# A convolution accumulated in PSUM banks, and half of a token mix moved from GpSimd to ScalarE

## The chip, the cores and the metric

The kernel runs on 1 core of one Trainium2 chip. The metric is device microseconds of one execution. Three runs of the kernel before took 1332.1, 1333.57 and 1333.91 us; the median is 1333.57 us.

## The reference

Three layers follow each other, all in fp32, on 8 batches of 576 tokens and 512 channels:

```python
scores = 0.125 * q @ k^T                        # 8 batches, 8 heads, 576 tokens, 64 wide
scores = where(scores >= max(scores) - tau, scores, -1e9)
x = softmax(scores) @ v                         # heads joined: 8 x 576 x 512

x_prev = x shifted by one token                 # first layer behind attention ("MoE 1")
xk = mu_k * x + (1 - mu_k) * x_prev
xr = mu_r * x + (1 - mu_r) * x_prev
v  = relu(xk @ w_k) ** 2 @ w_v                  # 512 -> 1024 -> 512
y  = sigmoid(xr @ w_r) * v

gate = sigmoid(sum over 5 taps of conv_w[k] * y shifted by 4 - k tokens)   # second layer
out  = (gate * (y @ w_val)) @ w_out
```

## The kernel before, in words

Channels lie on partitions, tokens along the free dimension. Behind attention the tokens of all batches (each padded by 4 zero columns) form one row of 4640, cut into 10 blocks of TW = 464. A block has KD = 4 chunks of 128 channels. Every matrix product is fp32 in three passes: each operand is split into a high part, rounded by ScalarE, and a low part (value minus high), subtracted on GpSimd (mostly) or VectorE; TensorE adds weight-high by data-high, weight-low by data-high and weight-high by data-low. So one product of a chunk with KD inputs is 12 matmuls of 464 columns, and a block of the second phase has 12 such products: four each with `w_r`, `w_val` and `w_out` (all at L549).

The first phase is attention with the products of `w_k` and `w_v` woven in. The second phase does, for each block of 464 tokens (`block2`):

- load `xt` (one buffer). For each chunk the shifted part of the mix `xf = omu * x_prev` on GpSimd (L596, in `shift_mix`), then `xf = mu * x + xf` on VectorE (L600, a SCALAR_TENSOR_TENSOR), the high part `xrh` on ScalarE (L611), the low part `xrl` on GpSimd (L614);
- four products with `w_r`; ScalarE takes the sigmoid out of PSUM into `gate` (L796);
- `y = gate * vt` on VectorE (L801), `yh` on ScalarE (L807), `yl` on GpSimd (L810);
- the convolution, for each chunk: tap 0 on ScalarE into the SBUF tile `gate` (L837), four taps on VectorE that read and write `gate` in place (L841), the sigmoid on ScalarE in place (L846);
- four products with `w_val` from `yh`, `yl`; VectorE multiplies the PSUM result by `gate` (L863); `gvh` on ScalarE (L869), `gvl` on GpSimd (L872);
- four products with `w_out`; ScalarE copies them out of PSUM (L888) and a DMA stores them.

PSUM has eight banks, named g0 to g7 in the second phase. Before, only TensorE writes them, and a product takes a free bank.

Nothing is ordered by hand. `Plan` records every operation with its engine, an assumed duration, its dependencies, a priority key (in units of one batch of attention) and tokens, which stand for buffers and banks that it takes and gives back. `Plan.order` plays this through once and so fixes, when the program is built, the order of the instructions on each engine. On the chip each engine runs its list strictly in order and waits on semaphores. A table of numbers (L148 to L165) sets the keys: how early score products, loads, mixes, taps and products are ranked.

Of the kernel before, what the change touches and what calls it, by code (L numbers as in the profile page):

```python
# [8 lines left out]
F32 = mybir.dt.float32  # L9
# [44 lines left out]
class Plan:  # L54
# [90 lines left out]

EARLY, QK_EARLY, T_LATE, EV_EARLY, AV_LATE = 0.1561, 0.0601, 0.0174, 4.8151, 0.1504  # L148
S3_CHUNKS = 54
MOE_LAG = 0.7824  # L150
MOE_STEP = 0.8138
KSTAGE = 4
KBUFS, XKBUFS = 10, 4
GATES = {"a": 1, "b": 3}
XRS = {"a": 1, "b": 1}
MIX_EARLY, SIDE_EARLY = 0.0845, -0.0305
W_KEY, W_STEP = 1.8064, 1.9807
V_KEY, V_STEP = 0.4408, 0.2458
R_AHEAD = 0
HOP = 240.0  # L160
VAL_LAG, OUT_LAG = -2.0743, 4.7957
LATE2, LOAD2, MIX2, CONV_LAG, THR_EARLY = 0.3053, 6.8806, 5.0887, 9.6459, 0.8081
MIX_AT = 133.6317
GUARD_POOL = 15
OUT_FETCH = 3.9825  # L165

SAME = {"dve": 130.0}
ENGINES = ("dma", "pe", "dve", "act", "pool", "none")
# [3 lines left out]
def body(ctx, tc, qka, qkb, vp, w_k, w_v, w_r, w_val, w_out, conv_w, par, out):  # L172
# [381 lines left out]
    def product(w, a, m, K, parts, prio, rel=(), cap=("mm",), each=()):  # L554


        t = {}

        def ps():
            return t["ps"]  # L560
        o = None
        for run, uses, first, end in mm3(ps, w, a, m, list(range(K))):
            def go(run=run, first=first):
                if first:
                    t["ps"] = bank(t["op"])
                run()
            deps = [o] + [parts[kc][at] for kc, at in uses]
            if first:
                deps += W_done[w][m // 4 * K:m // 4 * K + K]
                deps += [h for h, *_ in parts]  # L570
                if cap:
                    deps.append(last.get("m1"))
            o = op("pe", 198 * len(uses), go, deps, prio, acq=cap + (BANKS,) if first else (),
                   rel=(rel if end else ()) + sum((tuple(each) for _, at in uses if at), ()))
            if first:
                t["op"] = o
                if cap:
                    chain("m1", o)
        return o, ps, cap + (t["op"],)

    xm = {}

    def shift_mix(w, src, prio, tiles, pool_, tag, toks, eng, opened=None):

        t, parts, ends = {}, [], []
        for c in range(KD):
            f = {}
            got, ps = src(c), []  # L590
            o = None
            for x, (get, at, k, deps) in enumerate(got):
                def prev(c=c, f=f, get=get, at=at, k=k, x=x):
                    if x == 0:
                        f["f"] = pool_().tile([128, TW], F32, name="xf", tag="xf", bufs=2)
                    nc.gpsimd.tensor_scalar(out=f["f"][:, at:at + k], in0=get()[:, 0:k], scalar1=omu[w][:, c:c + 1],  # L596
                                            scalar2=1.0, op0=ALU.mult, op1=ALU.mult)

                def mix(c=c, f=f, get=get, at=at, k=k):
                    nc.vector.scalar_tensor_tensor(out=f["f"][:, at:at + k], in0=get()[:, 1:1 + k],  # L600
                                                   scalar=mu[w][:, c:c + 1], in1=f["f"][:, at:at + k],
                                                   op0=ALU.mult, op1=ALU.add)
# [133 lines left out]
    def after_first():  # L736
# [5 lines left out]
               rel=BANKS[4:] + ("mm", "mm"))  # L742
    end_1 = op("none", 0, after_first, v_kept[-KD:] + [W_done["v"][-1]] + W_done["out"], 0)
    tokens.update(xt=1, axr=XRS["a"], bxr=XRS["b"], rxf=2, agate=GATES["a"], bgate=GATES["b"],
                  vt=2, y=2, yh=2, gv=2, o=3)
    fetch_weight("r", end_a, -2)
    fetch_weight("val", end_a, -1)
    fetch_weight("out", end_1, B + MOE_LAG + OUT_FETCH)
# [1 line left out]
    def block2(n, base):  # L750
# [26 lines left out]
        def xr_tiles(c):  # L777
            if c == 0:
# [1 line left out]
            return [x[:, c, :] for x in t["xr"]]  # L780
        get, parts, ends = shift_mix("r", lambda c: [(lambda: t["xt"][:, c, :], 0, TW, (lx,))], se + MIX2, xr_tiles,
                                     lambda: pool["a"], "xr",
                                     ("rxf", lambda c: () if c else (xr_at + "xr",)), R_LO, xr_ready[xr_at])
        op("none", 0, lambda: None, [e[-1] for e in ends], 0, rel=("xt",))


# [1 line left out]
        for m in range(KD):  # L788
# [20 lines left out]
            def lo(m=m):  # L809
# [5 lines left out]
            o = chain("ymul", op("dve", 554, mul, (o, lv, last.get("ymul"), end_1), pr - LATE2,  # L815
                                 acq=("y",) if m == 0 else (), rel=("vt",) if m == KD - 1 else ()))
            h = chain("yh", op("act", 497, hi, (o, last.get("yh")), pr - LATE2, acq=("yh",) if m == 0 else ()))
            l = op("pool", 1155, lo, (h,), pr - LATE2)
# [14 lines left out]
        for c in range(KD):  # L833
            pr = base + CONV_LAG + c * u

            def tap0(c=c):
                nc.scalar.activation(out=t["gate"][:, c, :], in_=t["y"][:, c, 0:TW], func=AF.Copy,  # L837
                                     scale=cw[:, c, 0:1])

            def tap(c=c, k=1):  # L840
                nc.vector.scalar_tensor_tensor(out=t["gate"][:, c, :], in0=t["y"][:, c, k:k + TW],  # L841
                                               scalar=cw[:, c, k:k + 1], in1=t["gate"][:, c, :],
                                               op0=ALU.mult, op1=ALU.add)

# [108 lines left out]
```

## Time and profile before

| | |
|---|---|
| median of three runs | 1333.57 us (1332.1 to 1333.91) |
| the profiled execution | 1332.2 us, of it 1330.4 us from the first to the last instruction (the span) |
| busy share of the span | TensorE 94%, VectorE 77%, ScalarE 61%, GpSimd 59% |
| mean granted TensorE clock | 0.976 of full speed |
| HBM traffic | 95 GB/s over the span |

[...] The share over the whole span is a mean over stages with different limits, so the views below are cut by stage.

### The profile page before, as it was taken

The page shows a single profiled execution, that of the slowest core. Times are in us where ns is not written, and L with a number is a line of the kernel's source. Part 1 is how long each engine was busy: PE and PEld are TensorE (multiplying, and loading weights), DVE is VectorE, ACT ScalarE, POOL GpSimd, SP SyncE. Part 2 cuts the span into 40 slices and gives each one's busy share as a digit, 9 for nine tenths or more (in the row PEclk, how much of TensorE's full clock was granted, in tenths as well). Part 3 has the DMA queues.
Part 4 walks back from the last instruction along what each step waited for, and adds up shares of the span by engine and source line. Part 5 has one row for each costly group of instructions (what it writes and reads, how often), then busy time and mean ns, then how long its engine had stood idle before and what let it go on. Part 6 is the DMA issues. An engine that isn't in the chain of part 4 may idle for free.

```text
span 1330.4 us, 21096 instructions
## 1 busy us (share of the span) xinstructions
PE 1250.3 (94%) x7104; PEld 1046.7 (79%) x7104; DVE 1018.5 (77%) x2078; ACT 817.0 (61%) x1568; POOL 783.9 (59%) x1001
## 2 busy tenths in 40 slices
PE   5787999999999999999999999999998788999998
PEld 4565778877888778878888888888886677888887
DVE  7999898798797797888796886854419999776540
ACT  6888877676677676776775776653324443445442
POOL 6999767556566666457565465441217776565422
PEclk8889999999999999999999999999999888999999
DMA  6442422433323233224332212004124212221112
GB/s 233 126 143 84 137 74 69 147 105 101 111 78 123 85 110 113 83 74 128 101 125 86 77 65 80 20 24 179 58 90 148 80 61 96 91 86 58 43 43 100
DMA packets 51339, 127.57 MB, mean 96 GB/s; under 512 B 8608, under 2 KB 26144, under 8 KB 50464
## 3 DMA queue, kind: packets, MB, share of 16 engines
q1 hardware_dynamic: 51232, 126.23, 28.6%
q8 instruction: 57, 0.93, 0.3%
q14 instruction: 50, 0.41, 0.1%
HBM read 91.48 MB, written 34.73 MB: 95 GB/s over the span
## 4 chain that ended last, share of the span: by engine, by line
PE 53%; DVE 20%; POOL 9%; issue 8%; ACT 6%; DMA 3%; SPq 0%; POOLq 0%; DVEq 0%; ACTq 0%
PE g L549 31%; PE s L408 8%; PE g L513 7%; PE g L464 6%; DVE gate L841 4%; DVE p L434 4%; DVE sm L417 2%; PE g L516 2%; ACT p L430 2%; DVE xf L600 2%; POOL yl L810 2%; POOL p L447 2%; DVE kl L363 1%; DVE k L660 1%; POOL gvl L872 1%
## 5 line engine op out<-in xcount | busy, mean ns | idle before, releaser
L447 POOL TENSOR_SCALAR p<-p,sm 128x576 f32<-128x576 f32 x288 | 239.1, 834 | 159.9 <-DVE sm L444 75.9
L434 DVE SCALAR_TENSOR_TENSOR p<-s,sm,p 128x576 f32<-128x576 f32 x288 | 231.0, 811 | 47.3 <-ACT p L430 34.3
L417 DVE TENSOR_REDUCE sm<-s 128x1 f32<-128x576 f32 x288 | 213.8, 749 | 58.8 <-PE s L408 56.2
L430 ACT ACTIVATE p<-s,sm 128x576 f32<-128x576 f32 x288 | 213.2, 750 | 73.6 <-DVE sm L417 49.8
L408 PE MATMUL s<-qkh 128*128 128x288 f32 x640 | 209.6, 341 | 26.7 <-DVE p L434 17.4
L464 PE MATMUL g<-par_t,p 128*128 128x128 f32 (+1 forms) x1312 | 185.5, 278 | 24.7 <-POOL p L447 14.5
L464 PEld LDWEIGHTS g<-par_t,p 128*128 128x128 f32 (+1 forms) x1312 | 152.7, 141 | 41.3 <-POOL p L447 26.4
L408 PE MATMUL s<-kl,qkh 128*128 128x288 f32 x640 | 184.0, 301 | 0.9 <-DVE kl L363 0.9
L420 POOL TENSOR_SCALAR sm<-sm,gs 128x1 f32<-128x1 f32 x288 | 114.1, 398 | 119.5 <-DVE sm L417 76.6
L475 ACT ACTIVATE pt<-g 128x512 f32<-128x512 f32 x256 | 144.5, 606 | 26.4 <-PE g L464 26.2
L408 PEld LDWEIGHTS s<-qkh 128*128 128x128 f32 x640 | 123.9, 194 | 45.7 <-DVE p L434 15.9
L841 DVE SCALAR_TENSOR_TENSOR gate<-y,cw_t,gate 128x464 f32<-128x464 f32 x160 | 139.2, 922 | 15.5 <-ACT gate L837 15.1
L513 PE MATMUL g<-pt,v 128*64 128x320 f32 (+1 forms) x1024 | 142.7, 421 | 0.1
L408 PEld LDWEIGHTS s<-kl,qkh 128*128 128x128 f32 x640 | 124.6, 195 | 6.4 <-DVE kl L363 1.5
L549 PE MATMUL g<-xkh,w_k_hi 128*128 128x464 f32 x320 | 123.0, 384 | 0.2 <-ACT pt L475 0.2
L549 PE MATMUL g<-kh,w_v_hi 128*128 128x464 f32 x320 | 121.6, 380 | 0.0
L549 PE MATMUL g<-xkh,w_k_lo 128*128 128x464 f32 x320 | 119.1, 372 | 0.0
L549 PE MATMUL g<-kh,w_v_lo 128*128 128x464 f32 x320 | 119.1, 372 | 0.0
L513 PEld LDWEIGHTS g<-pt,v 128*64 128x64 f32 x1024 | 69.4, 139 | 56.7 <-issue 13.7
L369 POOL TENSOR_TENSOR qkh<-raw,qkh 64x576 fp32r<-64x576 f32 x64 | 94.8, 1481 | 11.3 <-ACT qkh L359 6.0
L614 POOL TENSOR_TENSOR xrl<-xf,xrh 128x464 fp32r<-128x464 f32 x40 | 59.0, 1490 | 65.8 <-ACT xrh L611 65.8
L810 POOL TENSOR_TENSOR yl<-y,yh 128x464 fp32r<-128x464 f32 x40 | 54.0, 1356 | 66.1 <-ACT yh L807 66.1
(99 smaller groups left out, 2679.7 us busy)
## 6 DMA issues: line engine op xcount, KB each, us to landing
raw<-in_qkb SPq DMA_DIRECT2D x32, 640.0 KB, 4.0
raw<-in_qka SPq DMA_DIRECT2D x32, 608.0 KB, 3.8
v<-in_vp SPq DMA_DIRECT2D x32, 320.0 KB, 3.2
x_d<-x SPq DMA_DIRECT2D x32, 290.0 KB, 3.6
v_d<-vo SPq DMA_DIRECT2D x40, 232.0 KB, 2.0
vt<-v_d SPq DMA_DIRECT2D x10, 928.0 KB, 4.6
stage<-in_w_v SPq DMA_DIRECT2D x8, 512.0 KB, 3.9
wst<-in_w_k SPq DMA_DIRECT2D x8, 512.0 KB, 6.0
```

The costliest lines, as they stand in the source:

```text
L369: nc.gpsimd.tensor_tensor(out=t["hi"][lo_rows, qs], in0=t["raw"][lo_rows, qs], in1=t["hi"][lo_rows, qs].bitcast(F32), op=ALU.subtract)
L408: nc.tensor.matmul(s_t[g][:, hh, 0:NT], lhsT=q, rhs=k, start=(i == 0), stop=(i == len(terms) - 1))
L417: nc.vector.tensor_reduce(out=sm[:, 0:1], in_=s_t[g][:, :, 0:NT], op=ALU.min, axis=AX.XY)
L420: nc.gpsimd.tensor_scalar(out=sm_t[g][:, 1:2], in0=sm_t[g][:, 0:1], scalar1=tau_t, scalar2=1.0, op0=ALU.add, op1=ALU.mult)
L430: nc.scalar.activation(out=view(), in_=s_t[g][:, :, 0:NT], func=AF.Exp, bias=sm_t[g][:, 0:1], scale=-1.0)
L434: nc.vector.scalar_tensor_tensor(out=view(), in0=s_t[g][:, :, 0:NT], scalar=sm[:, 1:2], in1=view(), op0=ALU.is_le, op1=ALU.mult, accum_out ...
L447: nc.gpsimd.tensor_scalar(out=view(), in0=view(), scalar1=sm_t[g][:, 3:4], scalar2=1.0, op0=ALU.mult, op1=ALU.mult)
L464: nc.tensor.transpose(ps[0:w, i * 128:(i + 1) * 128], in_=p_t[pi, j][:, p0:p0 + w], identity=ident)
L475: nc.scalar.activation(out=pt[:, head, :, q0:q0 + 128], in_=ps.rearrange("p (k q) -> p k q", k=4), func=AF.Copy)
L513: nc.tensor.matmul(acc[h * 64:h * 64 + 64, 0:n], lhsT=v[:, kc * 128 + h * 64:kc * 128 + h * 64 + 64], rhs=pt[:, h, kc, 0:n], start=(kc == ...
L549: nc.tensor.matmul(ps()[:, 0:TW], lhsT=W[w][wt][:, kc, m * 128:(m + 1) * 128].bitcast(F32R), rhs=a(at, kc), start=(i == 0 and x == 0), sto ...
L841: nc.vector.scalar_tensor_tensor(out=t["gate"][:, c, :], in0=t["y"][:, c, k:k + TW], scalar=cw[:, c, k:k + 1], in1=t["gate"][:, c, :], op0 ...
```

## The change

Two things in the second phase change their place.

- The convolution. Tap 0 writes a PSUM bank instead of `gate`, the four taps on VectorE read and write that bank in place, and the sigmoid reads the bank and writes `gate`. Each chunk's chain takes a bank token and one of `cv` = 3 tokens, and gives them back behind the sigmoid.
- The mix for `xr`. The shifted part is an activation with a scale on ScalarE that writes a PSUM bank, no longer a GpSimd instruction that writes `xf`; VectorE reads `xt` and that bank and writes `xf`. It takes a bank token and one of `xp` = 2 tokens until VectorE is done. The mix for `xk` in the first phase stays as it was.

The assumed durations of four operations and the table of keys change too, so the order on every engine is another one.

```diff
-S3_CHUNKS = 54
-MOE_LAG = 0.7824
+S3_CHUNKS = 45
+MOE_LAG = 0.7323
+CVB = 3
 ...
-    R_LO = {"pool": 1155}
+    R_LO = {"pool": 1300}
 ...
-    def shift_mix(w, src, prio, tiles, pool_, tag, toks, eng, opened=None):
+    def shift_mix(w, src, prio, tiles, pool_, tag, toks, eng, opened=None, psum=False):
 ...
                 def prev(c=c, f=f, get=get, at=at, k=k, x=x):
+                    if psum:
+                        f["p"] = bank(f["op"])[:, 0:TW]
+                        nc.scalar.activation(out=f["p"], in_=get()[:, 0:k], func=AF.Copy, scale=omu[w][:, c:c + 1])
+                        return
 ...
                 def mix(c=c, f=f, get=get, at=at, k=k):
+                    if psum:
+                        f["f"] = pool_().tile([128, TW], F32, name="xf", tag="xf", bufs=2)
                     nc.vector.scalar_tensor_tensor(out=f["f"][:, at:at + k], in0=get()[:, 1:1 + k],
-                                                   scalar=mu[w][:, c:c + 1], in1=f["f"][:, at:at + k],
+                                                   scalar=mu[w][:, c:c + 1], in1=f["p"][:, at:at + k],
                                                    op0=ALU.mult, op1=ALU.add)
 ...
+                if psum:
+                    o = f["op"] = chain("mix", op("act", 497, prev, first + [last.get("mix")], prio, acq=(BANKS, "xp")))
+                    ps.append(chain("mixd", op("dve", 130 + 1.04 * k, mix, (o, last.get("mixd")), prio, acq=toks[:1],
+                                               rel=(o, "xp"))))
+                    continue
 ...
-                  vt=2, y=2, yh=2, gv=2, o=3)
+                  vt=2, y=2, yh=2, gv=2, o=3, cv=CVB, xp=2)
 ...
-            def tap0(c=c):
-                nc.scalar.activation(out=t["gate"][:, c, :], in_=t["y"][:, c, 0:TW], func=AF.Copy,
-                                     scale=cw[:, c, 0:1])
+            def tap0(c=c, f=f):
+                f["ps"] = bank(f["op"])[:, 0:TW]
+                nc.scalar.activation(out=f["ps"], in_=t["y"][:, c, 0:TW], func=AF.Copy, scale=cw[:, c, 0:1])
 
-            def tap(c=c, k=1):
-                nc.vector.scalar_tensor_tensor(out=t["gate"][:, c, :], in0=t["y"][:, c, k:k + TW],
-                                               scalar=cw[:, c, k:k + 1], in1=t["gate"][:, c, :],
+            def tap(c=c, k=1, f=f):
+                nc.vector.scalar_tensor_tensor(out=f["ps"], in0=t["y"][:, c, k:k + TW],
+                                               scalar=cw[:, c, k:k + 1], in1=f["ps"],
                                                op0=ALU.mult, op1=ALU.add)
 
-            def sig2(c=c):
-                nc.scalar.activation(out=t["gate"][:, c, :], in_=t["gate"][:, c, :], func=AF.Sigmoid)
-            o = op("act", 574, tap0, (hd,), pr)
+            def sig2(c=c, f=f):
+                nc.scalar.activation(out=t["gate"][:, c, :], in_=f["ps"], func=AF.Sigmoid)
+            o = f["op"] = op("act", 574, tap0, (hd, last.get("tap0")), pr, acq=(BANKS, "cv"))
+            last["tap0"] = o
             for k in range(1, 5):
-                o = op("dve", 612, lambda c=c, k=k: tap(c, k), (o,), pr)
-            gates.append(op("act", 497, sig2, (o,), pr))
+                o = op("dve", 612, lambda c=c, k=k, tap=tap: tap(c, k), (o,), pr)
+            gates.append(op("act", 447, sig2, (o,), pr, rel=(f["op"], "cv")))
```

VectorE's list at the start of the second phase, from its first multiplication `y` on, before (L801 is `y`, L841 a tap, L600 the mix, L863 the multiplication of a `w_val` product by `gate`; the number behind a name is the buffer):

```order
L801 TENSOR_TENSOR y_11393<-gate_11214,vt_11367 128x464 x4
L801 TENSOR_TENSOR y_11444<-gate_11437,vt_11397 128x464
L841 SCALAR_TENSOR_TENSOR gate_11214<-y_11393,cw_t_87,gate_11214 128x464 x2
L600 SCALAR_TENSOR_TENSOR xf_11476<-xt_11424,par_t_83,xf_11476 128x464
L600 SCALAR_TENSOR_TENSOR xf_11484<-xt_11424,par_t_83,xf_11484 128x464
L841 SCALAR_TENSOR_TENSOR gate_11214<-y_11393,cw_t_87,gate_11214 128x464 x6
L600 SCALAR_TENSOR_TENSOR xf_11525<-xt_11424,par_t_83,xf_11525 128x464
L863 TENSOR_TENSOR gate_11214<-g0_11432,gate_11214 128x464
```

And the same place now (L813 is `y`, L855 a tap, L607 the mix, L878 the multiplication by `gate`; a name that begins with g0 to g7 is a PSUM bank):

```order
L813 TENSOR_TENSOR y_11403<-gate_11224,vt_11368 128x464 x4
L855 SCALAR_TENSOR_TENSOR g6_11452<-y_11403,cw_t_87,g6_11452 128x464
L855 SCALAR_TENSOR_TENSOR g5_11454<-y_11403,cw_t_87,g5_11454 128x464
L607 SCALAR_TENSOR_TENSOR xf_11473<-xt_11411,par_t_83,g3_11463 128x464
L855 SCALAR_TENSOR_TENSOR g6_11452<-y_11403,cw_t_87,g6_11452 128x464
L607 SCALAR_TENSOR_TENSOR xf_11491<-xt_11411,par_t_83,g0_11471 128x464
L813 TENSOR_TENSOR y_11495<-gate_11435,vt_11438 128x464
L855 SCALAR_TENSOR_TENSOR g6_11452<-y_11403,cw_t_87,g6_11452 128x464
L813 TENSOR_TENSOR y_11495<-gate_11435,vt_11438 128x464
L607 SCALAR_TENSOR_TENSOR xf_11524<-xt_11411,par_t_83,g1_11493 128x464
```

Of block 0's taps eight stood ahead of the third mix of block 2; now three stand there, and the `y` of block 1 have moved up between them. Two taps' banks and two mixes' banks are held at the same time.

ScalarE's list at its first taps 0, before (L837 is tap 0, L611 `xrh`, L846 the sigmoid of the convolution, L796 the sigmoid of a `w_r` product, L869 `gvh`):

```order
L837 ACTIVATE gate_11214<-y_11393,cw_t_87 128x464 x4
L611 ACTIVATE xrh_11497<-xf_11476 128x464
L611 ACTIVATE xrh_11497<-xf_11484 128x464
L846 ACTIVATE gate_11214<-gate_11214 128x464 x2
L796 ACTIVATE gate_11437<-g7_11417 128x464
L611 ACTIVATE xrh_11497<-xf_11525 128x464
L869 ACTIVATE gvh_11550<-gate_11214 128x464 x2
```

And now (L852 is tap 0, L597 the shifted part of the mix, L808 the sigmoid of a `w_r` product, L623 `xrh`, L819 `yh`):

```order
L852 ACTIVATE g6_11452<-y_11403,cw_t_87 128x464
L852 ACTIVATE g5_11454<-y_11403,cw_t_87 128x464
L597 ACTIVATE g3_11463<-xt_11411,omu_t_88 128x464
L597 ACTIVATE g0_11471<-xt_11411,omu_t_88 128x464
L808 ACTIVATE gate_11435<-g1_11429 128x464
L852 ACTIVATE g4_11480<-y_11403,cw_t_87 128x464
L623 ACTIVATE xrh_11488<-xf_11473 128x464
L597 ACTIVATE g1_11493<-xt_11411,omu_t_88 128x464
```

The four taps 0 of a block no longer stand together, and the shifted part of the mix, which waits for the load of `xt`, stands in ScalarE's list between them and the sigmoids.

## Rows read from the trace of the kernel before

**Rows 1.** Windows: engines' busy us (instructions), granted clock, DMA share, GB/s, by stage.

```profile
core 0: us, PE busy (x) PEld busy (x) DVE busy (x) ACT busy (x) POOL busy (x), PEclk, DMA share, GB/s
0.00:140.00 140.00, 104.35 (x610) 76.93 (x611) 125.21 (x293) 110.40 (x210) 119.28 (x166) 0.88 0.45 150
140.00:989.00 849.00, 832.19 (x5075) 696.72 (x5074) 656.72 (x1512) 558.65 (x1084) 470.63 (x674) 1.00 0.28 91
989.00:1010.00 21.00, 19.07 (x87) 15.68 (x87) 11.74 (x11) 10.47 (x19) 15.64 (x14) 1.00 0.79 293
1010.00:1120.00 110.00, 89.55 (x365) 74.73 (x364) 107.52 (x114) 47.57 (x89) 80.14 (x64) 0.88 0.21 70
1120.00:1326.20 206.20, 205.16 (x975) 182.69 (x973) 117.31 (x151) 89.34 (x168) 98.19 (x84) 1.00 0.21 72
1326.20:1330.40 4.20, 0.01 (x1) 0.00 (x0) 0.00 (x0) 0.56 (x1) 0.00 (x0) 0.85 0.29 113
```

**Rows 2.** Chain of waits, long pieces: start us, us, what.

```profile
1211.32 114.91 PE g L549 x549
```

**Rows 3.** Waits of TensorE, 950 to 1331 us: us in total, times, longest.

```profile
PE g L549 <- ACT yh L807: 17.3, 9, 3.5
PE g L549 <- POOL xrl L614: 3.4, 3, 2.1
```

**Rows 4.** Timeline of TensorE from 1056 us: start, us, instruction, idle before.

```profile
1057.32 0.48 PE L549 MATMUL g<-yh,w_val_hi 128*128 128x464 f32 x1 [2.03 <-ACT yh L807]
1061.52 0.76 PE L549 MATMUL g<-yh,w_val_hi 128*128 128x464 f32 x1 [3.51 <-ACT yh L807]
1064.01 0.59 PE L549 MATMUL g<-yh,w_val_hi 128*128 128x464 f32 x1
```

**Rows 5.** Single lines: duration ns min/median/max, first and last start us.

```profile
L841 DVE SCALAR_TENSOR_TENSOR gate<-y,cw_t,gate x160: 682/696/1678, 1006.7 to 1280.5; 128x464 f32<-128x464 f32 x160
L801 DVE TENSOR_TENSOR y<-gate,vt x40: 626/1510/1629, 996.9 to 1267.0; 128x464 f32<-128x464 f32 x40
L863 DVE TENSOR_TENSOR gate<-g,gate x40: 621/628/643, 1017.1 to 1281.9; 128x464 f32<-128x464 f32 x40
L660 DVE TENSOR_TENSOR k<-k x80: 614/642/2014, 155.4 to 966.0; 128x464 f32<-128x464 f32 x80
```

**Rows 6.** Timeline of VectorE and of GpSimd from 1021 us.

```profile
1021.36 4.67 DVE L841 SCALAR_TENSOR_TENSOR gate<-y,cw_t,gate 128x464 f32<-128x464 f32 x3
...
1022.44 1.55 POOL L614 TENSOR_TENSOR xrl<-xf,xrh 128x464 fp32r<-128x464 f32 x1
1023.96 1.58 POOL L810 TENSOR_TENSOR yl<-y,yh 128x464 fp32r<-128x464 f32 x1
```

**Rows 7.** Timeline of VectorE where GpSimd rests.

```profile
1246.63 1.92 DVE L841 SCALAR_TENSOR_TENSOR gate<-y,cw_t,gate 128x464 f32<-128x464 f32 x3
```

**Rows 8.** Windows of the taps alone (L841): VectorE busy, clock, DMA.

```profile
1010.00:1120.00 110.00, 67.23 (x66) 0.88 0.21 70
```

**Rows 9.** Windows of the mix alone (L600).

```profile
1010.00:1120.00 110.00, 18.34 (x17) 0.88 0.21 70
```

**Rows 10.** Windows of y alone (L801).

```profile
1010.00:1120.00 110.00, 16.67 (x15) 0.88 0.21 70
```

**Rows 11.** Windows of the multiplication by gate alone (L863).

```profile
1010.00:1120.00 110.00, 9.73 (x16) 0.88 0.21 70
```

**Rows 12.** Groups: names, shapes, count | busy us, mean ns | idle before.

```profile
L837 ACT ACTIVATE gate<-y,cw_t 128x464 f32<-128x464 f32 x40 | 24.6, 671 | 4.7 <-POOL y L826 4.1 <-POOL y L824 0.5
L596 POOL TENSOR_SCALAR xf<-xt,omu_t 128x464 f32<-128x464 f32 x40 | 38.6, 976 | 13.9 <-DMA xt<-x_d 13.9
```

**Rows 13.** Windows of the shifted part alone (L596): GpSimd busy, clock, DMA.

```profile
1010.00:1120.00 110.00, 18.41 (x18) 0.88 0.21 70
```

**Rows 14.** The first product of the first phase (last figures: first, last start).

```profile
L549 PE MATMUL g<-xkh,w_k_hi x320: 366/372/615, 144.1 to 963.8; 128*128 128x464 f32 x160
```

More of the change, by code (lines that the diff above doesn't have):

```diff
@@ L144, in order @@
         return out
-EARLY, QK_EARLY, T_LATE, EV_EARLY, AV_LATE = 0.1561, 0.0601, 0.0174, 4.8151, 0.1504
-S3_CHUNKS = 54
-MOE_LAG = 0.7824
-MOE_STEP = 0.8138
+EARLY, QK_EARLY, T_LATE, EV_EARLY, AV_LATE = 0.3412, 0.191, -0.1043, 3.5787, 0.083
+S3_CHUNKS = 45
+MOE_LAG = 0.7323
+MOE_STEP = 0.7954
 KSTAGE = 4
 KBUFS, XKBUFS = 10, 4
+CVB = 3
 GATES = {"a": 1, "b": 3}
 XRS = {"a": 1, "b": 1}
-MIX_EARLY, SIDE_EARLY = 0.0845, -0.0305
-W_KEY, W_STEP = 1.8064, 1.9807
-V_KEY, V_STEP = 0.4408, 0.2458
+MIX_EARLY, SIDE_EARLY = 0.5595, -0.1137
+W_KEY, W_STEP = 1.1719, 2.4131
+V_KEY, V_STEP = 1.1249, 0.0151
 R_AHEAD = 0
 HOP = 240.0
-VAL_LAG, OUT_LAG = -2.0743, 4.7957
-LATE2, LOAD2, MIX2, CONV_LAG, THR_EARLY = 0.3053, 6.8806, 5.0887, 9.6459, 0.8081
-MIX_AT = 133.6317
+VAL_LAG, OUT_LAG = 2.0619, 5.0024
+LATE2, LOAD2, MIX2, CONV_LAG, THR_EARLY = 1.1014, 10.4631, -0.7218, 10.0024, 0.6737
+MIX_AT = 334.259
 GUARD_POOL = 15
-OUT_FETCH = 3.9825
+OUT_FETCH = 4.3504
 SAME = {"dve": 130.0}
@@ L572, in product @@
                     deps.append(last.get("m1"))
-            o = op("pe", 198 * len(uses), go, deps, prio, acq=cap + (BANKS,) if first else (),
+            o = op("pe", 210 * len(uses), go, deps, prio, acq=cap + (BANKS,) if first else (),
                    rel=(rel if end else ()) + sum((tuple(each) for _, at in uses if at), ()))
@@ L593, in prev @@
                 def prev(c=c, f=f, get=get, at=at, k=k, x=x):
+                    if psum:
+                        f["p"] = bank(f["op"])[:, 0:TW]
+                        nc.scalar.activation(out=f["p"], in_=get()[:, 0:k], func=AF.Copy, scale=omu[w][:, c:c + 1])
+                        return
                     if x == 0:
-                        f["f"] = pool_().tile([128, TW], F32, name="xf", tag="xf", bufs=2)
+                        f["f"] = f["p"] = pool_().tile([128, TW], F32, name="xf", tag="xf", bufs=2)
                     nc.gpsimd.tensor_scalar(out=f["f"][:, at:at + k], in0=get()[:, 0:k], scalar1=omu[w][:, c:c + 1],
@@ L782, in block2 @@
                                      lambda: pool["a"], "xr",
-                                     ("rxf", lambda c: () if c else (xr_at + "xr",)), R_LO, xr_ready[xr_at])
+                                     ("rxf", lambda c: () if c else (xr_at + "xr",)), R_LO, xr_ready[xr_at], psum=True)
         op("none", 0, lambda: None, [e[-1] for e in ends], 0, rel=("xt",))
@@ L814, in block2 @@
             pr = base + m * u
-            o = chain("ymul", op("dve", 554, mul, (o, lv, last.get("ymul"), end_1), pr - LATE2,
+            o = chain("ymul", op("dve", 900, mul, (o, lv, last.get("ymul"), end_1), pr - LATE2,
                                  acq=("y",) if m == 0 else (), rel=("vt",) if m == KD - 1 else ()))
@@ L834, in block2 @@
             pr = base + CONV_LAG + c * u
-            def tap0(c=c):
-                nc.scalar.activation(out=t["gate"][:, c, :], in_=t["y"][:, c, 0:TW], func=AF.Copy,
-                                     scale=cw[:, c, 0:1])
-            def tap(c=c, k=1):
-                nc.vector.scalar_tensor_tensor(out=t["gate"][:, c, :], in0=t["y"][:, c, k:k + TW],
-                                               scalar=cw[:, c, k:k + 1], in1=t["gate"][:, c, :],
+            f = {}
+            def tap0(c=c, f=f):
[4 more added lines that the diff above has]
+                                               scalar=cw[:, c, k:k + 1], in1=f["ps"],
                                                op0=ALU.mult, op1=ALU.add)
-            def sig2(c=c):
-                nc.scalar.activation(out=t["gate"][:, c, :], in_=t["gate"][:, c, :], func=AF.Sigmoid)
-            o = op("act", 574, tap0, (hd,), pr)
+            def sig2(c=c, f=f):
+                nc.scalar.activation(out=t["gate"][:, c, :], in_=f["ps"], func=AF.Sigmoid)
+            o = f["op"] = op("act", 574, tap0, (hd, last.get("tap0")), pr, acq=(BANKS, "cv"))
+            last["tap0"] = o
             for k in range(1, 5):
-                o = op("dve", 612, lambda c=c, k=k: tap(c, k), (o,), pr)
-            gates.append(op("act", 497, sig2, (o,), pr))
+                o = op("dve", 612, lambda c=c, k=k, tap=tap: tap(c, k), (o,), pr)
+            gates.append(op("act", 447, sig2, (o,), pr, rel=(f["op"], "cv")))
         last["ydone"] = gates + [p_[1] for p_ in yparts]
```

## The prediction

> **What bounds the kernel now.** I read the windows by stage first [rows 1]. From 140 to 989 us, attention with the first layer, TensorE is busy 832.19 of 849 us at full clock: bound by TensorE, and the change can win little there. From 1120 to 1326.2 us it is busy 205.16 of 206.2: bound by it too. Two stages lose time. In the first 140 us TensorE has 104.35 us of work at clock 0.88, while VectorE (125.21) and GpSimd (119.28) are nearly full. And from 1010 to 1120 us, the start of the second phase, VectorE is busy 107.52 of 110 us and TensorE 89.55 at clock 0.88.
>
> What would that last stage take if nothing held TensorE? The chain of waits has a stretch of 549 second-phase matmuls in 114.91 us without a pause [rows 2], 0.2093 us each. The 365 matmuls of the stage make 76.4 us of that; it takes 110. So 33.6 us are lost: 110 - 89.55 = 20.4 us idle, and 89.55 - 76.4 = 13.1 us of slower matmuls. The waits name the holder: TensorE waits 17.3 us for `yh` [rows 3], which ScalarE makes from VectorE's `y`. The timeline shows two such waits, of 2.03 and 3.51 us, and behind them matmuls of 0.59 us where 0.37 is the median of others [rows 4, 14]: the clock goes down after TensorE has stood still.
>
> Why is VectorE full? A tap takes 0.682 us at least and up to 1.678; `y` 0.626 to 1.629, with a median of 1.510; but the multiplication by `gate`, which has one of its two tensors in PSUM, never leaves 0.621 to 0.643 [rows 5]. The timeline shows the reason: three taps take 4.67 us while GpSimd runs two subtractions of 1.55 and 1.58 us beside them [rows 6], and three taps take 1.92 us where GpSimd rests [rows 7]. A VectorE instruction with two tensors in SBUF waits for GpSimd's to end; one with a tensor in PSUM does not.
>
> **The change part by part.** All sums are against the profiled execution, 1332.2 us of which 1330.4 are the span; that is 1.4 us below the median of the runs shown, 1333.57.
>
> Taps. In the stage 66 taps take 67.23 us [rows 8], 1.02 each. Now each has one tensor in SBUF and one in PSUM and does not meet GpSimd. Undisturbed, three in a row take 1.92 us, the last one's 0.70 (the median of all) in it, so (1.92 - 0.70) / 2 = 0.61 from start to start [rows 5, 7]. A PSUM input adds little: 0.628 for the multiplication by `gate` against at least 0.614 for the same operation from SBUF [rows 5], 14 ns. No row shows VectorE writing PSUM, or reading and writing one bank at once. Bounds: 0.61 below, since each column still passes, and above the 1.02 of today, as if it read and wrote the bank in turns. I take 0.63, near the row that shares an operand in PSUM: 66 x 0.63 = 41.6 us.
>
> [...]
>
> Mix. 17 take 18.34 us [rows 9]; at 0.63 they make 10.7. `y` keeps two SBUF tensors and still meets GpSimd: 16.67 us for 15 [rows 10], left as it is, though GpSimd will be there less. The multiplication by `gate` keeps its 9.73 us [rows 11].
>
> VectorE's sum for the same work: 41.6 + 10.7 + 16.7 + 9.7 = 78.7 us instead of 107.5. TensorE needs 76.4. So the stage is balanced, and the larger is 78.7 us. The lists stay strictly in order, and `y`, mixes and taps are handed over between three engines; I allow 5 us for those gaps and for what clock they cost. The stage falls from 110 to 84 us: **-26 us**.
>
> ScalarE. 17 shifted parts come to it, with the form of tap 0, 0.671 us from SBUF to SBUF [rows 12]: 17 x 0.671 = 11.4 us on top of 47.57, 59 of 84 us, 70%. Writes of ScalarE into PSUM are not in the trace; even at 1 us each it would be 64.6 us, so the throughput is covered, the order not (rivals). GpSimd loses 18.41 us in the stage [rows 13] and keeps 61.7 of 84.
>
> Rest of the second phase. 989 to 1010 idles 1.9 us and 1120 to 1326 idles 1.0 [rows 1]: nothing to win, unchanged. The last 4.2 us, copying out and the store, stay.
>
> First phase. None of its operations changes, but its order does. The first product of `w_k`, today at 144.1 us [rows 14], moves in the list from behind 52 of 288 score chunks to behind 47; 144.1 / 52 = 2.8 us per chunk, so it comes 14 us earlier. TensorE runs at 104.35 / 140 = 75% there, and at less than full clock, so up to a quarter of the 14 us is saved if VectorE can feed it: I take **-3 us**, between +2 (VectorE is full there, and the splitting of weights still has to be done before) and -6.
>
> Sum: 1332.2 - 26 - 3 = 1303 us for an execution like the profiled one, 1304.5 with the 1.4 us to the median. I say 1304.
>
> **The rivals.**
>
> *Half of it is eaten by the order* (12%). The stage needs VectorE 78.7 and TensorE 76.4 us, so neither has slack, and every time one list waits for another it is lost on both. The lists show that `y` of block 2 on and the mixes stand between single taps of two or three chains. If it costs 15 to 25 us instead of 5, the result is 1314 to 1324. Against it: outside this stage VectorE has 43% slack, so nothing accumulates.
>
> *Taps in PSUM are no faster* (8%). At the upper bound 1.02, and with mixes as today, VectorE's sum is 67.3 + 18.3 + 26.4 = 112 us, and the stage stays at 110. What is left is the 3 us of the first phase and small change: 1328 to 1336. For it: no row shows the operation. Against it: a row with a PSUM input is steady at 0.628.
>
> *Banks and ScalarE become the bound: slower* (10%). Before, only products hold banks, and in the list a bank comes round after 6 or more products. Now up to 3 chains and 2 mixes hold one each, and 37 of the 120 second-phase products take a bank that was used two or three products, 5 to 7.5 us, before. Such a product starts only when the mix, the multiplication or the sigmoid that held its bank is through its in-order list. The shifted part also brings a wait along: GpSimd waited 13.9 us for the load of `xt` [rows 12]; on ScalarE the sigmoids, `yh` and `gvh` of all other blocks queue behind it, and TensorE waits for those. It would cost all through the second phase, 1340 matmuls or 112 products from 1010 us on. The gain of 29 us is gone at 0.26 us a product; at 0.4 us it is 1332 - 29 + 45 = 1348. Against it: ScalarE and VectorE are below 60% busy after 1120 us [rows 1], so both come to an evacuation soon. [...]
>
> *More than forecast* (4%): `y` gains too. With GpSimd's load down, 15 `y` at 0.63 save 7 us, and the first phase its 6: below 1292.
>
> **How the numbers follow.** The forecast has 66%, with a range of its own of 1292 to 1316 (gaps 0 to 14 us, first phase +2 to -6). For this kernel 0.2%, 2.7 us, is what can be told from no change. Faster: 66 + 12 + 4 and 3 of the 8 of dear taps, 85%. Within 0.2%: 4 of those 8. Slower: the 10 and the last 1, 11%. The range for 8 in 10 goes from 1291 over the half-eaten case to 1331, which leaves out the slower cases and the tails.
>
> **What would show it.** Right: taps at 0.69 to 0.72 us with a maximum near it, mixes the same, `y` still up to 1.6; between 1010 and 1120 us TensorE above 95% and the clock at 1.00; the second phase, from the last `w_v` product to the end, about 315 us instead of the 341 from 989 on; the first product of `w_k` near 130 us. Wrong: taps over 1 us without GpSimd beside them (second rival); TensorE's waits naming ScalarE's sigmoids or VectorE's multiplications, spread to the end (third); or a first phase that ends later than 989 us.

## The result and the profile after

The changed kernel takes 1295.98 us (median of four runs, 1294.72 to 1297.26) against 1332.84 (1332.1 to 1333.91) for the kernel before on the same chip: a ratio of 0.972, 95% interval 0.9706 to 0.974. It is faster, by 8 us more than the 1304 forecast, and inside the range of 1291 to 1331. The profiled execution took 1296.9 us, its span 1295.1.

First the windows by stage of the changed kernel, cut as in [rows 1]; the stage of 110 us that lost time is now gone by 1090.

```profile
core 0: us, PE busy (x) PEld busy (x) DVE busy (x) ACT busy (x) POOL busy (x), PEclk, DMA share, GB/s
0.00:140.00 140.00, 105.26 (x609) 77.64 (x611) 124.28 (x280) 110.14 (x209) 118.19 (x164) 0.91 0.44 145
140.00:991.00 851.00, 831.64 (x5068) 699.28 (x5065) 651.10 (x1533) 564.78 (x1092) 466.07 (x662) 1.00 0.28 92
991.00:1010.00 19.00, 19.00 (x90) 16.45 (x89) 10.37 (x14) 12.21 (x23) 11.54 (x10) 1.00 0.82 316
1010.00:1090.00 80.00, 79.85 (x381) 71.19 (x381) 77.84 (x125) 60.61 (x117) 54.17 (x49) 1.00 0.34 116
1090.00:1291.00 201.00, 200.92 (x963) 180.25 (x961) 87.67 (x137) 87.82 (x169) 76.89 (x69) 1.00 0.19 67
```

In the 80 us from 1010 on TensorE runs 381 matmuls at a granted clock of 1.00 and idles 0.15 us; before, 365 took 110 us at clock 0.88. VectorE is still 97% busy there, but now TensorE sets the pace. The first two rows read much as before.

The waits of TensorE between 950 us and the end are down to one, where [rows 3] had 17.3 us behind `yh` alone:

```profile
PE g L550 <- POOL xrl L626: 0.2, 1, 0.2
```

and the chain of waits ends in one piece, the second phase's matmuls without a pause:

```profile
1017.06 273.87 PE g L550 x1309
```

That is 0.2092 us each, the rate that [rows 2] had in its own free stretch. Single lines of VectorE and ScalarE (duration min/median/max in ns), to be laid beside [rows 5]; L855 is a tap, L607 the mix, L813 `y`, L878 the multiplication by `gate`, L597 the shifted part, now on ScalarE:

```profile
L855 DVE SCALAR_TENSOR_TENSOR g<-y,cw_t,g x160: 687/699/707, 1005.3 to 1233.0; 128x464 f32<-128x464 f32 x160
L607 DVE SCALAR_TENSOR_TENSOR xf<-xt,par_t,g x40: 680/690/700, 934.2 to 1159.2; 128x464 f32<-128x464 f32 x40
L813 DVE TENSOR_TENSOR y<-gate,vt x40: 629/643/1629, 999.2 to 1216.5; 128x464 f32<-128x464 f32 x40
L878 DVE TENSOR_TENSOR gate<-g,gate x40: 624/642/645, 1015.4 to 1261.0; 128x464 f32<-128x464 f32 x40
L597 ACT ACTIVATE g<-xt,omu_t x40: 632/638/653, 930.7 to 1138.9; 128x464 f32<-128x464 f32 x40
```

The four lines that touch PSUM spread over 21 ns at most from the shortest to the longest. `y`, which still has two tensors in SBUF, alone keeps the long tail to 1629 ns; its median fell from 1510 to 643 without its own instruction having changed (the new order does most of that, as the experiments show). The timeline shows VectorE and GpSimd side by side (start us, duration, engine, line, count, idle time before in brackets):

```profile
1025.70 0.92 DVE L813 TENSOR_TENSOR y<-gate,vt 128x464 f32<-128x464 f32 x1
1026.54 0.69 DVE L855 SCALAR_TENSOR_TENSOR g<-y,cw_t,g 128x464 f32<-128x464 f32 x1
1027.15 1.03 DVE L813 TENSOR_TENSOR y<-gate,vt 128x464 f32<-128x464 f32 x1
1032.58 1.91 DVE L855 SCALAR_TENSOR_TENSOR g<-y,cw_t,g 128x464 f32<-128x464 f32 x3
...
1024.93 2.75 POOL L626 TENSOR_TENSOR xrl<-xf,xrh 128x464 fp32r<-128x464 f32 x2 [0.20 <-ACT xrh L623]
1031.44 2.35 POOL L822 TENSOR_TENSOR yl<-y,yh 128x464 fp32r<-128x464 f32 x2 [1.65 <-ACT yh L819]
1033.76 1.19 POOL L626 TENSOR_TENSOR xrl<-xf,xrh 128x464 fp32r<-128x464 f32 x1
```

Three taps run in 1.91 us beside GpSimd's subtractions, as three did before only where GpSimd rested [rows 6, 7]; each of the two `y` beside such subtractions is stretched. The same holds over all 160 taps when the two engines' rows are laid over each other: before, the 55 taps that took over 1.1 times the shortest all overlapped a GpSimd instruction; now 74 taps overlap one and none takes more than 707 ns.

### The profile page after: what moved, and what is told of

It is laid out like the page before. It is cut to its first block, busy times and chain, and to the rows that moved or that the text cites. A ratio compares the mean times of both kernels' runs of the same rounds, so it can differ in the third digit from the quotient of the medians.

```text
span 1295.1 us, 21071 instructions
## 1 busy us (share of the span) xinstructions
PE 1236.7 (95%) x7104; PEld 1044.8 (81%) x7104; DVE 951.3 (73%) x2086; ACT 836.1 (65%) x1608; POOL 726.9 (56%) x953
## 5 line engine op out<-in xcount | busy, mean ns | idle before, releaser
L448 POOL TENSOR_SCALAR p<-p,sm 128x576 f32<-128x576 f32 x288 | 242.2, 845 | 154.0 <-DVE sm L445 89.9
L409 PE MATMUL s<-qkh 128*128 128x288 f32 x640 | 209.8, 342 | 31.3 <-DVE p L435 20.0
L465 PE MATMUL g<-par_t,p 128*128 128x128 f32 (+1 forms) x1312 | 189.2, 277 | 17.6 <-POOL p L448 11.8
L421 POOL TENSOR_SCALAR sm<-sm,gs 128x1 f32<-128x1 f32 x288 | 120.4, 420 | 119.0 <-DVE sm L418 72.5
L409 PEld LDWEIGHTS s<-qkh 128*128 128x128 f32 x640 | 124.2, 194 | 50.0 <-DVE p L435 22.5
L476 ACT ACTIVATE pt<-g 128x512 f32<-128x512 f32 x256 | 147.4, 604 | 25.0 <-PE g L465 24.0
L550 PE MATMUL g<-kh,w_v_hi 128*128 128x464 f32 x320 | 124.8, 390 | 2.4 <-ACT pt L476 2.2
L626 POOL TENSOR_TENSOR xrl<-xf,xrh 128x464 fp32r<-128x464 f32 x40 | 50.3, 1278 | 119.6 <-ACT xrh L623 88.7
L855 DVE SCALAR_TENSOR_TENSOR g<-y,cw_t,g 128x464 f32<-128x464 f32 x160 | 103.7, 699 | 6.7 <-ACT g L852 6.1
L370 POOL TENSOR_TENSOR qkh<-raw,qkh 64x576 fp32r<-64x576 f32 x64 | 98.0, 1531 | 12.9 <-ACT qkh L360 6.6
L887 POOL TENSOR_TENSOR gvl<-gate,gvh 128x464 fp32r<-128x464 f32 x40 | 47.1, 1204 | 71.2 <-PE g L550 55.9
```

What stands on the lines that cost most here:

```text
L370: nc.gpsimd.tensor_tensor(out=t["hi"][lo_rows, qs], in0=t["raw"][lo_rows, qs], in1=t["hi"][lo_rows, qs].bitcast(F32), op=ALU.subtract)
L409: nc.tensor.matmul(s_t[g][:, hh, 0:NT], lhsT=q, rhs=k, start=(i == 0), stop=(i == len(terms) - 1))
L421: nc.gpsimd.tensor_scalar(out=sm_t[g][:, 1:2], in0=sm_t[g][:, 0:1], scalar1=tau_t, scalar2=1.0, op0=ALU.add, op1=ALU.mult)
L448: nc.gpsimd.tensor_scalar(out=view(), in0=view(), scalar1=sm_t[g][:, 3:4], scalar2=1.0, op0=ALU.mult, op1=ALU.mult)
L465: nc.tensor.transpose(ps[0:w, i * 128:(i + 1) * 128], in_=p_t[pi, j][:, p0:p0 + w], identity=ident)
L476: nc.scalar.activation(out=pt[:, head, :, q0:q0 + 128], in_=ps.rearrange("p (k q) -> p k q", k=4), func=AF.Copy)
```

## Where the 35.3 us came from

The profiled executions differ by 35.3 us in span. I cut both at the start of the last `w_v` product, the end of the first phase. Its row before and after:

```profile
L549 PE MATMUL g<-kl,w_v_hi x320: 366/372/460, 219.9 to 988.4; 128*128 128x464 f32 x160
```

```profile
L550 PE MATMUL g<-kl,w_v_hi x320: 366/372/457, 209.0 to 991.1; 128*128 128x464 f32 x160
```

So the first phase ended 2.7 us later, and the second phase, from there to the end of the span, went from 342.0 to 304.0 us: 38.0 won. At 0.2093 us a matmul the second phase before had lost 33.6 us between 1010 and 1120, 21 - 87 x 0.2093 = 2.8 before that and 206.2 - 975 x 0.2093 = 2.1 behind it, 38.5 in all [rows 1, 2]. By that count nearly all that could come back came back.

## The experiments

Theory A: a VectorE instruction with two tensors in SBUF waits for GpSimd, and the gain comes from moving one operand of taps and mixes to PSUM. Theory B: it comes from the other order (the table of keys and the assumed durations). Each run below was timed beside the kernel before on its own chip (1331.8 to 1332.61 us). Beside the time I read from each profile the second phase alone, from the start of the last `w_v` product to the start of the last `w_out` product (337.4 us before, 299.4 after), since the first phase scatters by itself (985.0 to 991.1 us at its end with one and the same list, as shown below). There is one profile of each kernel. The last `w_out` product before and after:

```profile
L549 PE MATMUL g<-gvl,w_out_hi x160: 366/372/376, 1108.0 to 1325.8; 128*128 128x464 f32 x160
```

```profile
L550 PE MATMUL g<-gvl,w_out_hi x160: 366/372/376, 1074.4 to 1290.5; 128*128 128x464 f32 x160
```

**Taps back in SBUF, nothing else.** Three SBUF buffers in place of the three banks; the order on every engine is that of the changed kernel.

```diff
-                f["ps"] = bank(f["op"])[:, 0:TW]
+                f["ps"] = pool["b"].tile([128, TW], F32, name="cvs", tag="cvs", bufs=CVB)
```

> The changed kernel with its order untouched on every engine; only the bank that a convolution chain writes is an SBUF tile (three of them) instead of a PSUM bank. Theory A (the gain comes from VectorE no longer meeting GpSimd): taps go back to about 1.0 us on average between 1010 and 1090 us, VectorE falls behind by about 20 us there and TensorE waits again: 1311 to 1320 us. Theory B (the gain comes from the new order of the lists): at most 4 us are lost, 1296 to 1300 us.

1322.77 us (1321.79 to 1323.28), ratio 0.993 (0.9915 to 0.9944): on theory A's side, but 2.8 us above the range expected for it. The second phase takes 330.4 us, 31.0 more than with the banks. The single line of the taps, and TensorE's waits from 950 us on (us in total, times, longest):

```profile
L855 DVE SCALAR_TENSOR_TENSOR cvs<-y,cw_t,cvs x160: 683/696/1678, 999.3 to 1259.9; 128x464 f32<-128x464 f32 x160
```

```profile
PE g L550 <- DVE xf L607: 7.7, 3, 3.1
PE g L550 <- ACT gate L808: 6.8, 4, 3.7
PE g L550 <- DVE gate L878: 3.4, 2, 3.0
```

The maximum is 1678 ns again, as in [rows 5], and the mean goes from 699 to 934 (groups by shape: busy us, mean ns | idle before; with the banks, then without):

```profile
L855 DVE SCALAR_TENSOR_TENSOR g<-y,cw_t,g 128x464 f32<-128x464 f32 x160 | 103.7, 699 | 6.7 <-ACT g L852 6.1
L855 DVE SCALAR_TENSOR_TENSOR cvs<-y,cw_t,cvs 128x464 f32<-128x464 f32 x160 | 142.4, 934 | 7.4 <-ACT cvs L852 6.8
```

All 48 taps that took over 1.1 times the shortest overlap a GpSimd instruction. The timeline shows it with the same GpSimd work beside:

```profile
1035.49 7.27 DVE L855 SCALAR_TENSOR_TENSOR cvs<-y,cw_t,cvs 128x464 f32<-128x464 f32 x5
...
1036.05 3.15 POOL L626 TENSOR_TENSOR xrl<-xf,xrh 128x464 fp32r<-128x464 f32 x2
1039.16 3.10 POOL L822 TENSOR_TENSOR yl<-y,yh 128x464 fp32r<-128x464 f32 x2
```

Five taps take 7.27 us, 1.45 each, and GpSimd's subtractions take 1.55 to 1.58 each instead of 1.19: each engine pays. The windows show VectorE full (79.48 of 80 us) and TensorE idle for 15.3 us, at a lower clock:

```profile
1010.00:1090.00 80.00, 64.66 (x274) 54.44 (x275) 79.48 (x91) 47.73 (x89) 53.01 (x41) 0.94 0.25 84
```

**The mix's partner in SBUF, nothing else.** ScalarE still computes the shifted part, into two SBUF buffers; same order.

```diff
-                        f["p"] = bank(f["op"])[:, 0:TW]
+                        f["p"] = pool_().tile([128, TW], F32, name="xps", tag="xps", bufs=2)
```

> The changed kernel with its order untouched; only the shifted part of the mix, still on ScalarE, goes into an SBUF tile instead of a PSUM bank, so the 40 mixes on VectorE have two SBUF inputs again. Theory A: some 12 mixes in the full stretch of VectorE cost 0.4 us more each, about 5 us, 1299 to 1303 us. Theory B: no change, 1295 to 1298 us.

1300.55 us (1298.45 to 1305.26), ratio 0.9769 (0.9747 to 0.979); second phase 305.7, 6.3 more. The mixes are disturbed again, up to 1632 ns:

```profile
L607 DVE SCALAR_TENSOR_TENSOR xf<-xt,par_t,xps x40: 682/958/1632, 931.1 to 1162.0; 128x464 f32<-128x464 f32 x40
```

**Both in SBUF.** The convolution is in `gate` as before; same order.

```diff
-                        f["p"] = bank(f["op"])[:, 0:TW]
+                        f["p"] = pool_().tile([128, TW], F32, name="xps", tag="xps", bufs=2)
 ...
-                f["ps"] = bank(f["op"])[:, 0:TW]
+                f["ps"] = t["gate"][:, c, :]
```

> The changed kernel with its order untouched; taps in place in the SBUF tile of the gate and the shifted part of the mix in an SBUF tile, both still on the engines of the changed kernel. Theory A: the losses of the two add up, 1316 to 1326 us, more than two thirds of the gain. Theory B: at most 5 us are lost, up to 1301 us.

1329.27 us (1326.67 to 1330.14), ratio 0.9976 (0.9966 to 0.9986), 3.3 us above theory A's range; second phase 335.3 of before's 337.4. With the order and ScalarE's shifted part kept, but no operand in PSUM, all but 2 us of the second phase's gain is gone.

**The order alone.** The kernel before with the table of keys and the assumed durations of the changed one (the sigmoid of the convolution, which still reads SBUF here, keeps its own). A new table gives this kernel a new order, not exactly that of the changed kernel.

```diff
-S3_CHUNKS = 54
+S3_CHUNKS = 45
 ...
-    R_LO = {"pool": 1155}
+    R_LO = {"pool": 1300}
 ...
-            o = op("pe", 198 * len(uses), go, deps, prio, acq=cap + (BANKS,) if first else (),
+            o = op("pe", 210 * len(uses), go, deps, prio, acq=cap + (BANKS,) if first else (),
 ...
-            o = chain("ymul", op("dve", 554, mul, (o, lv, last.get("ymul"), end_1), pr - LATE2,
+            o = chain("ymul", op("dve", 900, mul, (o, lv, last.get("ymul"), end_1), pr - LATE2,
```

> The kernel before with all operations where they were (taps in SBUF, shifted part on GpSimd), but with the changed kernel's table of keys and its assumed durations, so a new order alone. Theory A: little of the gain, 1322 to 1340 us. Theory B: most of the gain of 37 us, below 1310 us.

1325.06 us (1323.2 to 1327.52), ratio 0.9949 (0.9931 to 0.9966). The new keys win 7 us by themselves: the second phase takes 330.7 us, taps still up to 1652 ns. They also shorten `y`, without any operand in PSUM (median 636 ns, before 1510):

```profile
L802 DVE TENSOR_TENSOR y<-gate,vt x40: 620/636/1634, 994.9 to 1248.0; 128x464 f32<-128x464 f32 x40
```

**The operations alone.** The counterpart: keys and durations of before, only the two moves.

```diff
-    R_LO = {"pool": 1300}
+    R_LO = {"pool": 1155}
 ...
-            o = op("pe", 210 * len(uses), go, deps, prio, acq=cap + (BANKS,) if first else (),
+            o = op("pe", 198 * len(uses), go, deps, prio, acq=cap + (BANKS,) if first else (),
 ...
```

(as against the changed kernel; the key table and the assumed duration of `y` are likewise those of before)

> The kernel before with nothing but the operations moved (convolution and shifted part into PSUM, the latter to ScalarE): keys and assumed durations of the kernel before. Theory A: the second phase takes 304 us as in the changed kernel and the first ends near 988 us as in the kernel before, so 1293 to 1297 us: the operations alone are the whole gain, the new keys add nothing on top. Rival (without the new keys TensorE waits at the start of the second phase): 1300 to 1312 us.

1296.46 us (1296.08 to 1298.48), ratio 0.9732 (0.9716 to 0.9749): not to be told from the changed kernel's 0.9706 to 0.974. The window from 1010 us, the two longest of TensorE's waits (all of them make 2.8 us), and `y`:

```profile
1010.00:1090.00 80.00, 78.52 (x375) 69.86 (x374) 73.36 (x117) 57.18 (x107) 51.01 (x47) 1.00 0.32 106
```

```profile
PE g L550 <- ACT gate L808: 1.2, 1, 1.2
PE g L550 <- POOL xrl L626: 1.0, 1, 1.0
```

```profile
L813 DVE TENSOR_TENSOR y<-gate,vt x40: 625/1284/1630, 996.4 to 1231.6; 128x464 f32<-128x464 f32 x40
```

The second phase takes 302.0 us with the old keys, 2.6 more than with the new ones. The keys were worth 7 us only while VectorE was late; the gains don't add up. Theory B falls, theory A stands. The median of `y` stays at 1284 ns here, so the fall to 643 in the changed kernel is mostly the new order's, and it is not needed for the gain.

**Each move alone** (both under the new order). Only the taps in PSUM, the mix of before on GpSimd and in SBUF:

```diff
-                                     ("rxf", lambda c: () if c else (xr_at + "xr",)), R_LO, xr_ready[xr_at], psum=True)
+                                     ("rxf", lambda c: () if c else (xr_at + "xr",)), R_LO, xr_ready[xr_at])
```

> The changed kernel with the mix as before (shifted part on GpSimd into SBUF, VectorE with two SBUF inputs), convolution in PSUM, keys of the changed kernel, order planned anew. Theory A (port): the mix is worth 5 to 12 us, as GpSimd gets 18 us more work in the full stretch and the mixes and y meet it again: 1301 to 1309 us. Rival (the convolution alone does it all): 1295 to 1299 us.

1305.02 us (1303.6 to 1310.9), ratio 0.9805 (0.9781 to 0.9829), second phase 308.2. ("Port" in the expectation stands for theory A; no run shows a port.) Only the mix moved, the convolution of before in `gate`:

```diff
-                f["ps"] = bank(f["op"])[:, 0:TW]
-                nc.scalar.activation(out=f["ps"], in_=t["y"][:, c, 0:TW], func=AF.Copy, scale=cw[:, c, 0:1])
+                nc.scalar.activation(out=t["gate"][:, c, :], in_=t["y"][:, c, 0:TW], func=AF.Copy,
+                                     scale=cw[:, c, 0:1])
 ...
```

(taps, sigmoid and tokens likewise)

> The changed kernel with the convolution as before (tap 0, taps and sigmoid in place in SBUF), shifted part on ScalarE into PSUM, keys of the changed kernel, order planned anew. Theory A: like the kernel with only the taps in SBUF, 1316 to 1326 us, since the order is nearly the same and the 160 taps meet GpSimd.

1318.02 us (1316.61 to 1319.89), ratio 0.9899 (0.9882 to 0.9915), second phase 322.2. From the 330.7 of the order alone, the taps win 22.5 us of the second phase and the mix 8.5; both together win 31.3. The two add up. This kernel does the same operations as the one with only the taps back in SBUF, in the same memories, yet its second phase is 8.2 us shorter (322.2 against 330.4). It is planned anew, without tokens for banks and chains, and works in `gate` and not in three buffers of its own; which of these wins the 8.2 us was not tested. So with a plan made for it, the taps' place in PSUM is worth 22.8 us of the second phase, and 31.0 only in the order of the changed kernel.

**More banks for the chains.**

```diff
-CVB = 3
+CVB = 5
```

> The changed kernel with five convolution chains allowed to hold a bank at once instead of three, order planned anew, so that with two mixes as little as one bank is left to TensorE. If banks are near their limit (my third rival), TensorE waits for them and it gets over 5 us slower, above 1301 us; if not: 1294 to 1299 us.

1295.05 us (1292.99 to 1297.62), ratio 0.9723 (0.9708 to 0.9738): no difference. Five banks for chains and two for mixes may now be away from the products. In the trace, from each first write to the last read, six were held at once for 24 us (in the changed kernel hardly ever more than five), and TensorE waits 1.2 us in all.

**The first phase's order, and one assumed duration.** Four runs on where the first phase ends: the whole old key table in the changed kernel, the old keys of the first phase alone, these with 198 ns instead of 210 assumed per matmul, and the changed kernel with 198. The edit of the third, which holds the others:

```diff
 ...
-S3_CHUNKS = 45
+S3_CHUNKS = 54
 ...
-W_KEY, W_STEP = 1.1719, 2.4131
+W_KEY, W_STEP = 1.8064, 1.9807
 ...
-            o = op("pe", 210 * len(uses), go, deps, prio, acq=cap + (BANKS,) if first else (),
+            o = op("pe", 198 * len(uses), go, deps, prio, acq=cap + (BANKS,) if first else (),
```

> The changed kernel's operations (taps and shifted part in PSUM, the latter on ScalarE) with the table of keys of the kernel before. Theory A: most of the gain remains, 1296 to 1310 us. Rival (the gain needs both, since the old order leaves TensorE waiting for y behind the taps, and the banks were not thought of in it): 1312 to 1325 us.

> The changed kernel with the keys of the kernel before for the first phase alone (score, exponential and transpose keys, number of early score chunks, lag and step of the first layer's products, the splitting of weights). The changed kernel's first phase ends 2.7 us later than that of the kernel before, by the last product of w_v; if the keys are the cause, the first phase ends near 988 us again and the second stays at 304 us: 1292 to 1295 us. If the second phase's place or the assumed durations are the cause: 1295 to 1298 us, no change.

> As the kernel with the old first-phase keys, whose first phase ended at 999.4 us, but with the assumed duration of a matmul back at 198 instead of 210. If the old keys go with the old duration (the plan then weaves the first layer's products as in the kernel before), the first phase ends near 988 us and the second takes its 304: 1293 to 1297 us. If the old keys themselves are at fault under the new operations: no change, 1304 to 1307 us.

> The changed kernel with the assumed duration of a matmul at 198 alone. Keys and duration fitted to each other: 3 to 10 us slower, 1299 to 1306 us, all of it in the first phase. If the duration does not matter with these keys: 1294 to 1298 us.

In that order 1307.67 us (ratio 0.9802 to 0.9831), 1305.58 (0.9787 to 0.9816), 1294.26 (0.9701 to 0.9734) and 1296.21 (0.9714 to 0.9743). The first lies in the range expected, but what it loses is not what either theory named: its first phase ends at 1002.0 us, and its second takes 300.0, as in the changed kernel. The second run missed both of its ranges; the other two came out in one of theirs. The last `w_v` product of the second and of the third of them:

```profile
L550 PE MATMUL g<-kl,w_v_hi x320: 366/372/460, 219.5 to 999.6; 128*128 128x464 f32 x160
```

```profile
L550 PE MATMUL g<-kl,w_v_hi x320: 366/372/460, 219.7 to 988.0; 128*128 128x464 f32 x160
```

With the old keys the first phase ends 11.6 us later when 210 is assumed, and the second phase is as long as in the changed kernel (299.4 and 299.8 us). With the new keys 198 or 210 makes no difference. This pair says only that such a number can cost 11 us through the order; which instructions of the first phase come too late stays open. The third has the lowest median of all, but its interval overlaps the changed kernel's: there is no version here that clearly beats it.

## Why the prediction was right

*What bounds the kernel, and taps.* Right, and shown: with the order held fixed and only the memory changed, the taps' mean is 934 or 699 ns and the second phase 330.4 or 299.4 us. The taps came out at 699 ns, inside the 0.69 to 0.72 named; in the stage 73 of them keep VectorE busy for 46.68 us, 0.64 each (forecast 0.63):

```profile
1010.00:1090.00 80.00, 46.68 (x73) 1.00 0.34 116
```

A PSUM operand cost little here where nothing disturbed: the shortest tap is 687 ns in place in a bank, 683 in SBUF. (The 14 ns that the prediction gives a PSUM input compare a median with a minimum; the two minima, 621 and 614 ns [rows 5], are 7 ns apart.) That a VectorE instruction with two tensors in SBUF waits for GpSimd's to end is in the trace of before: in [rows 6] the third tap ends at 1026.03 us, 0.49 behind GpSimd's second subtraction, and each of the 55 taps over 1.1 times the shortest ends 0.48 to 0.50 us behind the end of a GpSimd instruction. Whole instructions do not stand one behind the other even so: with the taps back in SBUF, where five taps met four subtractions, a tap took 1.45 us and a subtraction 1.56, and the undisturbed 0.61 and 1.19 would make 1.80 (an estimate from those rows).

*The size: -26 forecast, -38.0 measured for the second phase.* Three terms were too careful. The first is VectorE's sum of 78.7 us. I left `y` in it as it was, at 16.67 / 15 = 1.11 us [rows 10]; in the stage it now takes 14.36 us for 18, 0.80:

```profile
1010.00:1090.00 80.00, 14.36 (x18) 1.00 0.34 116
```

so VectorE's sum for the old stage's work is 66 x 0.64 = 42.2, 17 mixes at 13.75 / 20 = 0.69 or 11.7, 15 `y` at 0.80 or 12.0 and 16 multiplications at 8.89 / 14 = 0.635 or 10.2, together 76.1 us instead of 78.7: no longer above TensorE's 76.4. Even that is too much, since neighbours on VectorE overlap and such a sum counts the overlap twice: before, the four rows [rows 8 to 11] add up to 112.0 us where VectorE is busy for 107.52, and the prediction set its 78.7 beside that 107.5; after, they add up to 83.7 where it is busy for 77.84. By the busy time now, 77.84 us for 125 instructions, the 114 of the old stage would take 71.0 us, as an estimate. So the two engines were not as evenly matched as the prediction had it: VectorE had some 5 us to spare beside TensorE's 76.4. The second term is the 5 us allowed for hand-overs between the engines. They were not lost: TensorE idles 0.15 of 80 us. The stage's work therefore takes 76.5 us and not 84, 7.5 us more won. The third term is the 2.8 and 2.1 us on both sides of the stage that I called "nothing to win", in idle time and slower matmuls. They make 4.9 us by that count, where 4.5 are left to explain.

The fourth rival named the `y` term; that it was part of the likeliest case I had not seen. Two things shorten it, and the runs separate them only in part: its median over all blocks, 1510 ns before, is 1284 with the operations alone and 636 with the new keys alone.

*First phase: -3 forecast, +2.7 measured; the saving is not seen.* The first product of `w_k` starts at 131.9 us, near the 130 named, 12.2 us earlier than in [rows 14]:

```profile
L550 PE MATMUL g<-xkh,w_k_hi x320: 366/372/734, 131.9 to 967.4; 128*128 128x464 f32 x160
```

But its end at 991.1 us is later than 989, which I had named as a sign of being wrong. One trace does not decide it: four kernels with the same first-phase list end it at 985.0, 986.6, 988.0 and 991.1 us, more apart than the term is large. All nine traces with the new first-phase keys have a mean of 988.0, and three with the old keys and 198 ns end at 988.0 to 988.5. So of the 12 us at the start nothing shows at the end, and neither does the quarter that was to be saved. That the whole came within 8 us is in part luck, since the misses run against each other: 12 us too little in the second phase, 5.7 too much in the first.

*Half eaten by the order* did not happen: 0.2 us of waits of TensorE with the new keys, 2.8 with the old ones.

*Taps in PSUM no faster* fell with the 699 ns.

*Banks and ScalarE become the bound* fell twice: in the changed kernel TensorE waits for neither ScalarE's sigmoids nor the multiplications, and more banks for the chains change nothing. The wait that I feared for ScalarE is there, 7.7 us for the load of `xt` in the groups by shape (busy us, mean ns | idle before), and TensorE does not come to wait for it:

```profile
L597 ACT ACTIVATE g<-xt,omu_t 128x464 f32<-128x464 f32 x40 | 24.7, 641 | 7.8 <-DMA xt<-x_d 7.7
```

In this phase, where a product of 12 matmuls takes 2.5 us, lending out up to five of the eight banks cost nothing that can be measured: TensorE waits 0.2 us in all, for `xrl`, and with five chains allowed instead of three the time is 1295.05 us against 1295.98.

## What to carry to other kernels

Where VectorE runs instructions with two SBUF tensors beside a busy GpSimd, read their minimum, median and maximum: a maximum far above a steady minimum, at times when GpSimd runs, said here that they hold each other up (taps of 0.682 to 1.678 us), and one operand in PSUM, even accumulated in place, took it away (0.687 to 0.707). Before you call two engines balanced, hold the sum of single lines against the busy time of the engine: here neighbours overlap, and the sum was too large (112.0 us where VectorE was busy for 107.52). Where a line that you did not touch gets faster too, find out which part of the change did it. An order or a table of keys that won time while an engine was late may be worth nothing once it is not, as the 7 us here: test it again without the cause.

## What was not expected of the hardware

- VectorE reading and writing the same bank in place cost 4 to 5 ns more than SBUF here without disturbance: 687 against 682 or 683 ns at the least, for 464 columns.
- ScalarE was quicker into PSUM: tap 0 takes 646 ns there on the mean, 671 into SBUF [rows 12], and 676 in the kernel with the taps back in SBUF.
- GpSimd gains too. Its subtraction `xrl` fell from a mean of 1490 ns to 1278, and is at 1371 with the taps back in SBUF.
- The mean granted clock of the stage went from 0.88 to 1.00 with no idle time left (0.15 us); in the kernel with taps in SBUF, where TensorE idles 15.3 of the 80 us from 1010 on, it is 0.94. Before, it did not fall behind every wait: it is 1.00 from 1054 to 1058 us, with the wait of 2.03 us [rows 4] in it, 0.68 from 1058 to 1062, with that of 3.51 us, and 0.50 from 1062 to 1066, with TensorE busy throughout. Of the 33.6 us 13.1 were busy time beyond 76.4, won back without any change to the matmuls. How much of it the clock made, and how much the longer single matmuls behind a wait (0.48 and 0.76 us at the two waits of [rows 4], where 0.37 is the median), was not separated; 76.4 at a clock of 0.88 would be 86.8, some 10 us more, as an estimate.
